# Scores of four chunks as three products of high and low parts, longer planned loads of q and k, and early weights from the thirtieth group on

## The chip, the cores and the metric

The kernel runs on one core of one Trainium2 chip. The metric is the device time of one execution in microseconds; the kernel before takes 701.42 us (median of 3 runs, 701.08 to 701.65).

The core has a matrix engine (TensorE, PE in the rows, with its weight loads shown apart as PEld), a vector engine (VectorE, DVE), a scalar engine (ScalarE, ACT), GpSimd (POOL) and SyncE (SP). POOL, SP and ACT also issue DMAs. Each engine works through its own list of instructions in order.

## What is computed

An attention with heads mixed before and after the softmax, and two feed-forward layers behind it:

```python
scores = scale * np.matmul(q, k.transpose(0, 1, 3, 2))      # 2 batches, 12 heads, 448 x 448, depth 64
scores = np.einsum('bhij,hg->bgij', scores, w_pre)
scores = scores - np.max(scores, axis=-1, keepdims=True)
attn = np.exp(scores)
attn = attn / (np.sum(attn, axis=-1, keepdims=True) + 1e-09)
attn = np.einsum('bhij,hg->bgij', attn, w_post)
x = np.matmul(attn, v)                                      # then 896 tokens x 768
h = x @ moe_w_in;  x = (h / (1 + np.exp(-1.702 * h))) @ moe_w_out
h = x @ moe2_w_in; x = (P(h) / (Q(h) + 1e-06)) @ moe2_w_out # P cubic, Q quadratic in |h|
```

The weights arrive as 64-bit numbers and are turned into float32 on the chip.

## The kernel before

**Attention.** The 448 query rows of a batch are cut into chunks of 120, 120, 120 and 88 rows: chunks 0 to 3 are of batch 0, chunks 4 to 7 of batch 1. The *scores* of a chunk (`scores`, L353) are computed for two heads at a time: q and k hold one head in partitions 0 to 63 and the other in 64 to 127, so that a pair is two float32 matmuls of 64 rows, on the two halves of the array, into the two banks of a tile `mm`. There are six pairs in a chunk. From chunk 2 on two pairs are issued one behind the other, as one block, so a chunk has three blocks. `scores_out` (L382, mostly on ACT) copies a pair to a tile S. SP then *regroups* (`regroup`, L391): one DMA for each group of 10 query rows (8 in the last group of a batch) moves all 12 heads of those rows from S into a tile T of 120 partitions. There are 90 groups, 12 for a chunk of 120 and 9 for one of 88, and ten T tiles.

For each group: `pre` (L397, PE) mixes the heads; `rowmax` (L403, DVE) and `expo` (L408, ACT) make the exponentials E; `norm` (L414, mostly DVE) the reciprocal of the sum and the scaled mixing matrix W and rest R; `post` (L443, PE, the matmuls of L449 and L452) mixes again and transposes; `post_out` (L454, mostly ACT) copies that to the tile AT of the chunk. When a chunk is done, `av` (L463, the matmuls of L475) multiplies with v and `x_part` (L485) splits the result into a rounded part (float32r) and the rest.

**Where S lies.** `place` (L314) gives each chunk a home for its scores: a tile S of its own, or one of two larger tiles that the feed-forward part needs only later (S2: the tag x1, S3: the tag wu). A chunk may write its scores to a place when all regroups of the chunk before it there are done (the mark `rgdone`, L597).

**Feed-forward.** `up` and `down` (L707, L775) take a weight and an activation as a high and a low float32r part each and sum three products: high by high, low by high, high by low (L715 to L717, L784 to L786).

**Weights.** A weight block is loaded by POOL (`w_load`, L659), taken through five conversions, one on ACT (`w_mag`, L667) and four on DVE (`w_bits`, L671), and split. The first 32 blocks of the second layer are converted ahead of time and stored to memory (`ahead`, L841); the first 12 of these (`EARLY`, L69) are spread over the attention groups, the others over the first layer. Six blocks of the first layer are also converted in the attention (`in_att`, L850).

**What sets the order.** A planner (`Plan`, L78) takes every step with its engine, its planned duration, its dependences, its buffers and a rank, runs a list schedule with these planned times when the program is built, and emits each engine's instructions in the order that comes out. Ranks count in groups: `RANK` (L34) says how many groups ahead of (negative) or behind its own group a step stands. A DMA step has a planned lag until it lands (`DMA_LAG`, L30). On the chip nothing is moved: an engine whose next instruction is not ready waits, and what stands behind it waits too.

The steps of the scores, the copies and the loads are made here:

```python
step(("kld", b, hp), "sp", 640 if b else 480, [("scdone", b * NC - 1)] if b else [], ...)      # L540
d0 = [("qld", ci), ("kld", b, hp | two)] + ([("sc", ci, hp - 1)] if two and hp % 2 else [])    # L562
step(("sc", ci, hp), "pe", 755, d0, rk, scores, ci, hp, take=["mm"], need=...)                 # L564
e = (NG - 12) * (j + 0.5) / EARLY + RANK["ahead"]                                              # L861
```

Of the kernel before, what the change touches and what calls it, by code (L numbers as in the profile page):

```python
# [29 lines left out]
DMA_LAG = 3500  # L30
RG_LAG = 5000
W_LAG = 5200

RANK = dict(k=-45, q=-45, v=-45, sc=-14, sco=-14, rg=-37, pre=-3, max=-3, exp=-6, n0=-9, n1=-9, n2=-4, n3=-4, post=1, phi=-4)  # L34
# [25 lines left out]
RB = 3  # L60
TAIL = 2
SINGLE = {0: (2, 3), 1: (0, 1)}
# [6 lines left out]
EARLY = 12  # L69
# [159 lines left out]
def row_groups(M):  # L229

    n = M // (2 * IS)
    left = M - 2 * n * IS
    out = []
    for g in range(2 * n):
        out.append((range(g, 2 * n * IS, 2 * n), g // 2 * IS + g % 2 * (n * IS + left)))
    return out + ([(range(M - left, M), n * IS)] if left else [])
# [3 lines left out]
def talking_heads_then_two_ffn(ctx: ExitStack, tc: tile.TileContext, q, k, v, wpre, wpost, win1, wout1, win2, wout2, ab, out):  # L240
# [12 lines left out]
    def psum(b, *n):  # L253
        return banks[b][plan.bank[n, b]]
# [59 lines left out]
    def place(ci):  # L314
        return ("S", "S2", "S3", "S2", "S", "S", "S3", "S")[ci]
# [7 lines left out]
    def load_k(b, hp):  # L323
        if hp == 0:
            t_["k", b] = ap1.tile([128, NP, S], F32, tag="k", name=f"k{b}")
        sp.dma_start(t_["k", b][:, hp], k[b, :, hp])

# [25 lines left out]
    def scores(ci, hp):  # L353
        b, c = chunks[ci]
        M = CHUNKS[c][1]
        p = t_["sc", ci, hp] = psum("mm", "sc", ci, hp)
        for o in range(2):
            r = slice(o * 64, o * 64 + 64)
            pe.matmul(p[:M, o, :S], t_["q", ci][r, hp, :M], t_["k", b][r, hp], start=True, stop=True)
# [80 lines left out]
    def alone(t):  # L440
        return t == last[groups[t][0]] and groups[t][1] % 2 == 0
# [11 lines left out]

    def post_out(t, eng):  # L454
        ci, gi, n, off = groups[t]
        if gi == 0:
            t_["AT", ci] = ap1.tile([128, NJ, H, IC], F32, tag="AT", bufs=2, name=f"AT{ci}")
        at = t_["AT", ci]
        p = t_["post", t][:, : NJ * IC].rearrange("p (j g i) -> p j g i", j=NJ, g=H)
        js = slice(0, NJ if gi % 2 or alone(t) else JM)  # L460
        cast(eng, at[:, js, :, off : off + n], p[:, js, :, :n])

    def av(ci, a):  # L463
        b, c = chunks[ci]
        M = CHUNKS[c][1]
        at, vt = t_["AT", ci], t_["v", b]
        y = t_["av", ci, a] = psum("bk", "av", ci, a)
        ev = M // (2 * IS) * IS
        parts = [(vt[:, jc], at[:, jc], 0, M) for jc in range(JM)]
        parts += [(vz[:, 0], at[:, JM, :, M - ev :], 0, ev), (vz[:, 1], at[:, JM, :, ev:], ev, M - ev)]  # L470
        for i in range(3):
            for k, (w, x, c0, n) in enumerate(parts):
                for o in range(2):
                    h = (3 * a + i) * 2 + o
                    pe.matmul(  # L475
                        y[o * 64 : o * 64 + 64, i * IC + c0 : i * IC + c0 + n],
                        w[:, h * D : h * D + D],
                        x[:, h, :n],
                        start=k == 0,
                        stop=k > JM,  # L480
                    )
# [3 lines left out]
    def x_part(ci, a, rest):  # L485
# [8 lines left out]
        else:  # L494
# [4 lines left out]
            **dict(mm=2, bk=4, T=TB, E=4, W=3, R=RB, sm=4, q=2, S=1, S2=1, S3=1, AT=2, k=1, v=1),  # L499
# [29 lines left out]
    def mark(name, deps, give):  # L529
        plan.add(name, (), deps, 0, give=give)  # L530
# [6 lines left out]
    for b in range(B):  # L537
        f0 = first[b * NC]
        for hp in range(NP):
            step(("kld", b, hp), "sp", 640 if b else 480, [("scdone", b * NC - 1)] if b else [], f0 + RANK["k"] + 0.01 * hp, load_k, b, hp, take=[] if hp else ["k"], lag=DMA_LAG)  # L540
        for jc in range(NJ):
            d0 = [("av", b * NC - 1, 1)] if b else [("vhold",)]
            step(("vld", b, jc), "sp" if b else "pool", 1280, d0, f0 + RANK["v"] + RANK["step_v"] * jc, load_v, b, jc, take=["v"] if b and not jc else [], lag=DMA_LAG)
    for ci, (b, c) in enumerate(chunks):
# [4 lines left out]
        step(("qld", ci), "sp" if ci else "act", 450 if ci else 890, d0, f0 + RANK["q"] - {1: 9.4, 2: 12.5}.get(ci, 0), load_q, ci, take=["q"], lag=DMA_LAG)  # L549
        for hp in range(NP):  # L550
# [11 lines left out]
            d0 = [("qld", ci), ("kld", b, hp | two)] + ([("sc", ci, hp - 1)] if two and hp % 2 else [])  # L562
            rk = -99 if two and hp % 2 else f0 + RANK["sc"] + 0.1 * hp
            step(("sc", ci, hp), "pe", 755, d0, rk, scores, ci, hp, take=["mm"], need=2 if two and hp % 2 == 0 else 1)  # L564
# [11 lines left out]
        mark(("scdone", ci), [("sc", ci, hp) for hp in range(NP)] + [("sc1", ci, hp) for hp in SINGLE.get(ci, ())], [("q", ("qld", ci))] + ([("k", ("kld", b, 0))] if end_b else []))  # L576
# [31 lines left out]
    mark(("late_s",), [("rgdone", 6)], [("wu", "late_s")] * 3)  # L608
# [246 lines left out]
    for key, us in uses.items():  # L855
# [3 lines left out]
        if key in ahead:  # L859
            j = ahead.index(key)  # L860
            e = (NG - 12) * (j + 0.5) / EARLY + RANK["ahead"]  # L861
# [21 lines left out]
    for L in range(2):  # L883
        for ft in range(NF):
            qq = ft // FQ
            for hf in range(2):
# [21 lines left out]
                if L == 0:  # L908
                    step(G, "act", 424, [u, ("exp", NG - 1)], p + RANK["gates"], gelu, key, take=["t0"], give=[bank])
                    step(("ghi",) + key, copying(S, "ghi0"), 0, [G] + g0, p + RANK["ghi0"], g_part, L, ft, hf, None, False, take=gt_)  # L910
                    step(("g",) + key, joining(S, "glo0"), 0, [("ghi",) + key], p + RANK["glo0"], g_part, L, ft, hf, None, True, give=[("t0", G)])
                else:
                    step(G, "act", 500, [u], p + RANK["gates"], cubic, key, take=["t0"])
# [109 lines left out]
```

## Time and profile of the kernel before

| | |
|---|---|
| median of the runs | 701.42 us (701.08 to 701.65, 3 runs) |
| the profiled execution | 700.76 us |
| its span, first to last instruction | 699.0 us |
| PE busy in the span | 694.0 us (99%) |
| DVE busy | 515.0 us (74%) |
| ACT busy | 459.5 us (66%) |
| POOL busy | 225.1 us (32%) |
| granted clock | 1.000 throughout |

The span is that of one execution, recorded by the profiler; 1.76 us of that execution's time lie outside it. Busy is the share of time in which an engine has an instruction in work; since matmuls overlap one another in the pipeline, a matmul's recorded duration is longer than the distance from its start to the next one's, and it is the distances between starts that add up to time on PE. The attention takes the first 234 us; the feed-forward layers the rest.

### The profile page before, as it was taken

Reading aid. Unit: us, or ns where it says so; the run is one execution under the profiler, and the core shown is the slowest. Engines: PE = TensorE matmul, PEld = TensorE weight load, DVE = VectorE, ACT = ScalarE, POOL = GpSimd, SP = SyncE. Lnnn points to the kernel's source line nnn. Section 1 sums busy time; section 2 is a strip of 40 time slices with the busy share of each in tenths; the row PEclk is TensorE's granted clock in tenths of the full one; section 3 lists DMA queues with packets and bytes.
Section 4 is the critical chain, followed back from the end, with each engine's and each line's share of the span. In section 5 each row is a group of like instructions: output and inputs, shape, how many; then the busy total and the mean of one; then the engine's idle time right before and its main releaser. Section 6 shows DMA issues by size and latency. Waiting matters only on the chain.

```text
span 699.0 us, 11972 instructions
## 1 busy us (share of the span) xinstructions
PE 694.0 (99%) x4292; PEld 594.1 (85%) x4292; DVE 515.0 (74%) x1101; ACT 459.5 (66%) x868; POOL 225.1 (32%) x361
## 2 busy tenths in 40 slices
PE   9999999999999999999999999999999999999998
PEld 4676767766769999999999999999999999999997
DVE  4688668567887596676787878859987387579952
ACT  4878677777685466665645554659898687488630
POOL 0411221120203255556465555412222222321320
PEclk9999999999999999999999999999999999999999
DMA  6886774864453487978889888755535544833563
GB/s 229 240 272 213 233 219 179 268 222 152 127 148 124 168 241 182 284 213 236 225 232 262 224 215 236 199 140 121 113 70 119 137 105 95 171 89 90 143 159 121
DMA packets 49961, 126.15 MB, mean 180 GB/s; under 512 B 7630, under 2 KB 21646, under 8 KB 49902
## 3 DMA queue, kind: packets, MB, share of 16 engines
q0 software_dynamic: 32480, 95.97, 51.1%
q1 hardware_dynamic: 17134, 29.05, 12.5%
q8 instruction: 34, 0.56, 0.3%
q10 hardware_dynamic: 288, 0.37, 0.1%
q14 instruction: 25, 0.20, 0.1%
HBM read 69.78 MB, written 13.24 MB: 119 GB/s over the span
## 4 chain that ended last, share of the span: by engine, by line
PE 70%; DMA 1%; ACT 0%; DVE 0%; issue 0%; ACTq 0%
PE bk L715 11%; PE mm L786 11%; PE mm L785 11%; PE mm L784 11%; PE bk L717 11%; PE bk L716 11%; PE bk L475 1%; PE bk L449 1%; DMA rawk<-in_wout_dram 1%; PE bk L400 1%; PE bk L452 0%; ACT wmk L669 0%; ACT AT L266 0%; DVE yt L274 0%; ACTq L669 0%
## 5 line engine op out<-in xcount | busy, mean ns | idle before, releaser
L785 PE MATMUL mm<-g,wd 128*128 128x448 f32 (+1 forms) x388 | 141.0, 363 | 0.0
L786 PE MATMUL mm<-g,wd 128*128 128x448 f32 (+1 forms) x388 | 141.0, 363 | 0.0
L784 PE MATMUL mm<-g,wd 128*128 128x448 f32 (+1 forms) x388 | 140.9, 363 | 0.0
L664 POOL DMA_DIRECT2D rawk<-in_win_dram x96 | 54.2, 593 | 172.9 <-ACT E L412 34.0
L449 PEld LDWEIGHTS bk<-W,E 120*128 120x128 f32 x540 | 72.2, 191 | 33.5 <-issue 21.6
L400 PE MATMUL bk<-T,wpr 120*120 120x448 f32 x180 | 81.5, 547 | 0.1
L785 PEld LDWEIGHTS mm<-g,wd 128*128 128x128 f32 x388 | 72.9, 188 | 5.7
L784 PEld LDWEIGHTS mm<-g,wd 128*128 128x128 f32 x388 | 72.9, 188 | 5.7
L786 PEld LDWEIGHTS mm<-g,wd 128*128 128x128 f32 x388 | 72.9, 188 | 5.6
L449 PE MATMUL bk<-W,E 120*128 120x120 f32 x540 | 76.0, 277 | 0.0
L406 DVE TENSOR_REDUCE sm<-bk 120x1 f32<-120x448 f32 (+1 forms) x90 | 55.8, 621 | 22.2 <-PE bk L400 20.8
L715 PE MATMUL bk<-xh,wu 128*128 128x448 f32 x192 | 70.5, 367 | 0.0
L715 PE MATMUL bk<-xn,wu 128*128 128x448 f32 x192 | 70.1, 365 | 0.0
L717 PE MATMUL bk<-xh,wu 128*128 128x448 f32 x192 | 70.1, 365 | 0.0
L716 PE MATMUL bk<-xn,wu 128*128 128x448 f32 x192 | 70.1, 365 | 0.0
L717 PE MATMUL bk<-xn,wu 128*128 128x448 f32 x192 | 70.1, 365 | 0.0
L716 PE MATMUL bk<-xh,wu 128*128 128x448 f32 x192 | 70.1, 365 | 0.0
L736 DVE SCALAR_TENSOR_TENSOR t<-t,cab,bk 128x448 f32<-128x448 f32 x64 | 43.5, 679 | 28.1 <-ACT t L732 21.4
L412 ACT ACTIVATE E<-bk,sm 120x448 f32<-120x448 f32 (+1 forms) x90 | 56.4, 627 | 6.9 <-PE bk L449 3.4
L266 ACT ACTIVATE AT<-bk 128x360 f32<-128x360 f32 (+2 forms) x83 | 43.3, 528 | 26.6 <-PE bk L452 15.7
L274 DVE TENSOR_TENSOR yt<-mm,yt 128x896 f32<-128x896 f32 (+2 forms) x44 | 40.4, 918 | 25.0 <-PE mm L786 24.8
L664 POOL DMA_DIRECT2D rawk<-in_wout_dram x56 | 32.3, 607 | 73.1 <-issue 19.9
(118 smaller groups left out, 1434.1 us busy)
## 6 DMA issues: line engine op xcount, KB each, us to landing
rawk<-in_win_dram POOLq DMA_DIRECT2D x96, 256.0 KB, 4.0
T<-S SPq DMA_DIRECT2D x88, 210.0 KB
rawk<-in_wout_dram POOLq DMA_DIRECT2D x56, 256.0 KB, 4.2
raw<-in_wout_dram POOLq DMA_DIRECT2D x40, 256.0 KB, 4.7
wd<-wm POOLq DMA_DIRECT2D x19, 256.0 KB, 4.9
d1u<-wmk POOLq DMA_DIRECT2D x24, 192.0 KB, 4.2
rawk<-d1u POOLq DMA_DIRECT2D x12, 384.0 KB, 4.1
wu<-rawk POOLq DMA_DIRECT2D x12, 384.0 KB, 4.2
```

Source lines behind the costliest of these rows:

```text
L400: pe.matmul(p[:K, :S], wpr[:K, :K], t_["T", t][:K], start=True, stop=True)
L406: dve.tensor_reduce(t_["sm", t][:K, 0:1], t_["pre", t][:K, :S], AX.X, ALU.max, negate=True)
L412: act.activation(t_["E", t][:K], t_["pre", t][:K, :S], AF.Exp, bias=sm[:K, 0:1], scale=1.0, accum_out=sm[:K, 1:2])
L449: pe.matmul(o, t_["E", t][:K, jc * 128 : jc * 128 + 128], t_["W", t][:K], start=True, stop=True)
L664: pool.dma_start(r[:, c : c + 256], src[:, c : c + 256])
L715: pe.matmul(p[:, :S], w[:, 0, ws], x[:, 0, kk], start=kk == 0, stop=False)
L716: pe.matmul(p[:, :S], w[:, 1, ws], x[:, 0, kk], start=False, stop=False)
L717: pe.matmul(p[:, :S], w[:, 0, ws], x[:, 1, kk], start=False, stop=kk == KK - 1)
L736: dve.scalar_tensor_tensor(t, t, col(i), t_[("h",) + key][:, :S], ALU.add, ALU.mult)
L784: pe.matmul(p[:, hf, :n], w[:, 0, ms], gt[:, 0, i, cs], start=i == 0, stop=False)
L785: pe.matmul(p[:, hf, :n], w[:, 1, ms], gt[:, 0, i, cs], start=False, stop=False)
L786: pe.matmul(p[:, hf, :n], w[:, 0, ms], gt[:, 1, i, cs], start=False, stop=i == FQ - 1)
```

## The change

- **Scores of chunks 3 to 6** (`SPLIT`): q and k are split into a high part rounded to float32r and a low part, the rest. ACT makes the high parts (`khi`, `qhi`), DVE the low ones (`klo`, `qlo`). Each pair is then three float32r products per half instead of one float32 product per half: high by high, high by low, low by high. The planned duration on PE is 610 instead of 755. k is split in six steps for each batch, q in one for each chunk.
- **Room.** The split k of batch 0 lies in S2's tile, that of batch 1 in S3's. `PLACES` changes: chunks 0, 3, 5, 6 and 7 use S, chunks 1 and 4 S2, chunk 2 S3. The split q has one buffer, as large as what the two AT tiles lose: AT holds, for each head, seven strips of half a chunk's columns instead of four of a chunk's, and the two rows of `vz` are exchanged to match, as is the order of the rows of q.
- **Loads.** k of batch 1 may be loaded when k of batch 0 has been split and chunks 0 to 2 are scored (it was: when chunk 3 was scored). The planned lag of a load is 9500 for q from chunk 3 on and 7500 for k of batch 1 (both were 3500).
- **Early weights.** 13 blocks instead of 12, with ranks spread from group 30 on instead of from the first.
- **Planned time** of the two first activations behind a table load: 1300 more. The first weights of the first layer get their tile when the scores of chunk 6 are done (it was: when its regroups were).

```diff
+Q_LAG, K_LAG = 9500, 7500
+TABLE = 1300
...
-RANK = dict(k=-45, q=-45, v=-45, sc=-14, sco=-14, rg=-37, pre=-3, max=-3, exp=-6, n0=-9, n1=-9, n2=-4, n3=-4, post=1, phi=-4)
+RANK = dict(kh=-15, k=-45, q=-45, v=-45, sc=-14, sco=-14, rg=-37, pre=-3, max=-3, exp=-6, n0=-9, n1=-9, n2=-4, n3=-4, post=1, phi=-4)
...
+STRIPS = 2 * JM + 1
+SPLIT = (3, 4, 5, 6)
+QB = 1
+WAIT = (1,), (2,)
+PLACES = "S", "S2", "S3", "S", "S2", "S", "S", "S"
...
-EARLY = 12
+EARLY = 13
+AFTER = 30
...
-        out.append((range(g, 2 * n * IS, 2 * n), g // 2 * IS + g % 2 * (n * IS + left)))
+        out.append((range(g, 2 * n * IS, 2 * n), g // 2 * IS + (1 - g % 2) * (n * IS + left)))
...
-        return ("S", "S2", "S3", "S2", "S", "S", "S3", "S")[ci]
+        return PLACES[ci]
...
+
+    def q_part(ci, rest):
+        if rest:
+            sub(dve, t_["qh", ci][:, 1], t_["q", ci], f(t_["qh", ci][:, 0]))
+        else:
+            t_["qh", ci] = ap1.tile([128, 2, NP, IC], F32R, tag="qh", bufs=QB, name=f"qh{ci}")
+            cast(act, t_["qh", ci][:, 0], t_["q", ci])
+
+    def k_part(b, hp, rest):
+        if rest:
+            sub(dve, t_["kh", b][:, 1, hp], t_["k", b][:, hp], f(t_["kh", b][:, 0, hp]))
+            return
+        if hp == 0 and b == 0:
+            t_["kh", b] = keep.tile([128, 2, KK, S], F32R, tag="x1", name="kh0")
+        elif hp == 0:
+            x = keep.tile([128, H * S], F32R, tag="wu", name="kh1")
+            t_["kh", b] = x.rearrange("p (a h s) -> p a h s", a=2, h=NP)
+        cast(act, t_["kh", b][:, 0, hp], t_["k", b][:, hp])
...
+        if ci in SPLIT:
+            qs, kh = t_["qh", ci], t_["kh", b]
+            terms = ((0, 0), (0, 1), (1, 0))
+            for i, (x, y) in enumerate(terms):
+                for o in range(2):
+                    r = slice(o * 64, o * 64 + 64)
+                    pe.matmul(p[:M, o, :S], qs[r, x, hp, :M], kh[r, y, hp], start=i == 0, stop=i == 2)
+            return
...
+    def strip(ci):
+        M = CHUNKS[chunks[ci][1]][1]
+        return M - M // (2 * IS) * IS
+
...
-            t_["AT", ci] = ap1.tile([128, NJ, H, IC], F32, tag="AT", bufs=2, name=f"AT{ci}")
-        at = t_["AT", ci]
-        p = t_["post", t][:, : NJ * IC].rearrange("p (j g i) -> p j g i", j=NJ, g=H)
-        js = slice(0, NJ if gi % 2 or alone(t) else JM)
-        cast(eng, at[:, js, :, off : off + n], p[:, js, :, :n])
+            t_["AT", ci] = ap1.tile([128, H * STRIPS * IC // 2], F32, tag="AT", bufs=2, name=f"AT{ci}")
+        w = strip(ci)
+        at = t_["AT", ci][:, : H * STRIPS * w].rearrange("p (g s u) -> p g s u", s=STRIPS, u=w)
+        p = t_["post", t][:, : NJ * IC].rearrange("p (j g i) -> p g j i", j=NJ, g=H)
+        if gi % 2 or alone(t):
+            cast(eng, at[:, :, ::2, off : off + n], p[:, :, :, :n])
+        else:
+            cast(eng, at[:, :, 1::2, off - w : off - w + n], p[:, :, :JM, :n])
...
-        at, vt = t_["AT", ci], t_["v", b]
+        vt = t_["v", b]
...
-        ev = M // (2 * IS) * IS
-        parts = [(vt[:, jc], at[:, jc], 0, M) for jc in range(JM)]
-        parts += [(vz[:, 0], at[:, JM, :, M - ev :], 0, ev), (vz[:, 1], at[:, JM, :, ev:], ev, M - ev)]
+        st = strip(ci)
+        at = t_["AT", ci][:, : H * STRIPS * st].rearrange("p (g c) -> p g c", g=H)
+        parts = [(vt[:, jc], at[:, :, 2 * jc * st :], 0, M) for jc in range(JM)]
+        parts += [(vz[:, 1], at[:, :, 2 * JM * st :], 0, st), (vz[:, 0], at[:, :, 2 * JM * st :], st, M - st)]
...
-            **dict(mm=2, bk=4, T=TB, E=4, W=3, R=RB, sm=4, q=2, S=1, S2=1, S3=1, AT=2, k=1, v=1),
+            **dict(mm=2, bk=4, T=TB, E=4, W=3, R=RB, sm=4, q=2, qh=QB, S=1, S2=1, S3=1, AT=2, k=1, v=1),
...
-            step(("kld", b, hp), "sp", 640 if b else 480, [("scdone", b * NC - 1)] if b else [], f0 + RANK["k"] + 0.01 * hp, load_k, b, hp, take=[] if hp else ["k"], lag=DMA_LAG)
+            step(("kld", b, hp), "sp", 640 if b else 480, ([("kld", b, 0)] if hp else [("scdone", 0)]) if b else [], f0 + RANK["k"] + 0.01 * hp, load_k, b, hp, take=[] if hp else ["k"], lag=K_LAG if b else DMA_LAG)
+        mine = [ci for ci in SPLIT if ci // NC == b]
+        for hp in range(NP if mine else 0):
+            rk = first[mine[0]] + RANK["kh"] + 0.1 * hp
+            step(("khi", b, hp), "act", 585, [("kld", b, hp)] + ([("khi", b, 0)] if hp else [("rgdone", c) for c in WAIT[b]]), rk, k_part, b, hp, False, take=[] if hp else ["S3" if b else "S2"])
+            step(("klo", b, hp), "dve", 560, [("khi", b, hp)], rk + 0.05, k_part, b, hp, True)
+        plain = [ci for ci in range(b * NC, b * NC + NC) if ci not in SPLIT]
+        mark(("kend", b), [("klo", b, hp) for hp in range(NP if mine else 0)] + [("scdone", ci) for ci in plain], [("k", ("kld", b, 0))])
+        if mine:
+            mark(("khend", b), [("scdone", ci) for ci in mine], [("S3" if b else "S2", ("khi", b, 0))])
...
-        step(("qld", ci), "sp" if ci else "act", 450 if ci else 890, d0, f0 + RANK["q"] - {1: 9.4, 2: 12.5}.get(ci, 0), load_q, ci, take=["q"], lag=DMA_LAG)
+        step(("qld", ci), "sp" if ci else "act", 450 if ci else 890, d0, f0 + RANK["q"] - {1: 9.4, 2: 12.5}.get(ci, 0), load_q, ci, take=["q"], lag=Q_LAG if ci > 2 else DMA_LAG)
+        if ci in SPLIT:
+            rk = f0 + RANK["kh"]
+            step(("qhi", ci), "act", 800, [("qld", ci)], rk, q_part, ci, False, take=["qh"])
+            step(("qlo", ci), "dve", 910, [("qhi", ci)], rk, q_part, ci, True, give=[("q", ("qld", ci))])
...
-            d0 = [("qld", ci), ("kld", b, hp | two)] + ([("sc", ci, hp - 1)] if two and hp % 2 else [])
+            split = ci in SPLIT
+            d0 = [("qlo", ci), ("klo", b, hp | two)] if split else [("qld", ci), ("kld", b, hp | two)]
+            d0 += ([("sc", ci, hp - 1)] if two and hp % 2 else [])
...
-            step(("sc", ci, hp), "pe", 755, d0, rk, scores, ci, hp, take=["mm"], need=2 if two and hp % 2 == 0 else 1)
+            step(("sc", ci, hp), "pe", 610 if split else 755, d0, rk, scores, ci, hp, take=["mm"], need=2 if two and hp % 2 == 0 else 1)
...
-        mark(("scdone", ci), [("sc", ci, hp) for hp in range(NP)] + [("sc1", ci, hp) for hp in SINGLE.get(ci, ())], [("q", ("qld", ci))] + ([("k", ("kld", b, 0))] if end_b else []))
+        mark(("scdone", ci), [("sc", ci, hp) for hp in range(NP)] + [("sc1", ci, hp) for hp in SINGLE.get(ci, ())], [("qh", ("qhi", ci)) if split else ("q", ("qld", ci))])
...
-    mark(("late_s",), [("rgdone", 6)], [("wu", "late_s")] * 3)
+    mark(("late_s",), [("khend", 1)], [("wu", "late_s")] * 3)
...
-            e = (NG - 12) * (j + 0.5) / EARLY + RANK["ahead"]
+            e = AFTER + (NG - 12 - AFTER) * (j + 0.5) / EARLY + RANK["ahead"]
...
-                    step(G, "act", 424, [u, ("exp", NG - 1)], p + RANK["gates"], gelu, key, take=["t0"], give=[bank])
+                    step(G, "act", 424 + TABLE * (ft == hf == 0), [u, ("exp", NG - 1)], p + RANK["gates"], gelu, key, take=["t0"], give=[bank])
...
-                    step(G, "act", 500, [u], p + RANK["gates"], cubic, key, take=["t0"])
+                    step(G, "act", 500 + TABLE * (ft == hf == 0), [u], p + RANK["gates"], cubic, key, take=["t0"])
...
```

## Rows read from the trace of the kernel before

**Rows 1.** The page's totals: busy us, share of the span, instructions, by engine

```profile
PE 694.0 (99%) x4292; PEld 594.1 (85%) x4292; DVE 515.0 (74%) x1101; ACT 459.5 (66%) x868; POOL 225.1 (32%) x361
```

**Rows 2.** Waits of PE: line, releaser, us in total, times, longest us

```profile
PE bk L260 <- DVE warm L279: 1.2, 1, 1.2
PE mm L359 <- ACT S L266: 0.3, 1, 0.3
```

**Rows 3.** Windows: stretch, length, each engine's busy us (instructions), granted clock, DMA share, GB/s

```profile
20.00:100.00 80.00, 80.00 (x627) 55.30 (x627) 61.51 (x206) 61.43 (x146) 22.25 (x42) 1.00 0.74 228
100.00:230.00 130.00, 129.86 (x1210) 97.30 (x1212) 95.09 (x302) 91.53 (x217) 23.25 (x43) 1.00 0.55 183
180.00:200.00 20.00, 20.00 (x204) 15.29 (x204) 18.59 (x53) 15.02 (x37) 3.21 (x6) 1.00 0.50 151
240.00:690.00 450.00, 450.00 (x2222) 417.00 (x2221) 341.51 (x563) 289.84 (x479) 175.97 (x268) 1.00 0.66 172
```

**Rows 4.** Timeline, 65.6 to 68.2: start us, us, engine, line, output<-inputs, shape, records

```profile
65.31 0.92 PE L400 MATMUL bk<-T,wpr 120*120 120x448 f32 x2
...
66.15 0.23 PEld L359 LDWEIGHTS mm<-k,q 64*88 64x88 f32 x4 [0.66 <-issue]
66.15 1.74 PE L359 MATMUL mm<-k,q 64*88 64x448 f32 x8
...
66.60 0.16 PEld L359 LDWEIGHTS mm<-k,q 64*88 64x88 f32 x2 [0.22 <-issue]
...
66.98 0.16 PEld L359 LDWEIGHTS mm<-k,q 64*88 64x88 f32 x2 [0.22 <-issue]
...
67.82 0.59 PE L449 MATMUL bk<-W,E 120*128 120x120 f32 x3
```

**Rows 5.** Timeline of PE, 299.70 to 302.14: first and last of thirteen starts

```profile
299.70 0.37 PE L716 MATMUL bk<-xh,wu 128*128 128x448 f32 x1
...
302.14 0.36 PE L785 MATMUL mm<-g,wd 128*128 128x448 f32 x1
```

**Rows 6.** Timeline of PE in the product with v: two neighbouring stretches

```profile
73.44 0.40 PE L475 MATMUL bk<-AT,vz 128*64 128x60 f32 x8
73.66 0.79 PE L475 MATMUL bk<-AT,v 128*64 128x120 f32 x12
```

**Rows 7.** Groups by line, 234 to 690: count, busy us, mean ns

```profile
L266 ACT ACTIVATE g<-t 128x448 fp32r<-128x448 f32 x61 | 35.0, 574 | 8.0 <-DVE t L756 7.1
...
L266 ACT ACTIVATE wu<-rawk 128x768 fp32r<-128x768 f32 x10 | 8.3, 834 | 0.0
...
L271 DVE TENSOR_TENSOR g<-t,g 128x448 fp32r<-128x448 f32 x64 | 39.7, 621 | 12.5 <-ACT g L266 11.8
...
L271 DVE TENSOR_TENSOR wu<-wmk,wu 128x768 fp32r<-128x768 f32 x1 | 1.0, 953 | 0.0
```

**Rows 8.** Windows of the converted weights alone (tile wmk): busy us (instructions)

```profile
20.00:85.00 65.00, 11.94 (x16) 3.64 (x4) 4.31 (x8) 1.00 0.75 237
85.00:100.00 15.00, 5.18 (x8) 1.56 (x2) 1.61 (x3) 1.00 0.67 186
100.00:230.00 130.00, 36.00 (x53) 10.64 (x13) 5.96 (x11) 1.00 0.55 183
```

**Rows 9.** The chain of waits, 196 to 207: start us, us, what

```profile
197.35 6.37 DMA rawk<-in_wout_dram
...
203.83 0.67 ACT wmk L669
...
205.02 1.76 PE bk L400 x4
```

**Rows 10.** Timeline of SP, 116 to 134: regroups around the scores of chunk 5

```profile
116.09 0.77 SPq L395 DMA_DIRECT2D T<-S  x1
...
133.21 0.86 SPq L395 DMA_DIRECT2D T<-S  x1
```

**Rows 11.** Timeline of PE at 144.54: the first pre of chunk 5

```profile
144.54 0.92 PE L400 MATMUL bk<-T,wpr 120*120 120x448 f32 x2
```

## The prediction

> **What bounds the kernel now.** I read the totals first: PE is busy 99% of the span, DVE 74%, ACT 66% [rows 1]. A busy PE may still be waiting inside its pipeline, so the second view is who PE waited for: in the whole span 1.2 us for the first memset, and behind that no wait on another engine above 0.3 us [rows 2]. [...] So time is the sum of PE's own work nearly from end to end: an edit that takes work from PE is worth its full length, and an edit on another engine costs nothing until PE waits for it. The reader should also see in [rows 3] how close that is: DVE has 18.59 of 20 us of work from 180 to 200 and PE still does not wait.
>
> **What a block of scores costs now.** The fourth view is the timeline around one block of two pairs [rows 4]. Its eight matmul records (two passes for each float32 product, for each half, for each pair) start at 66.15 and what follows starts at 67.82. The two halves run side by side: loads come in twos, at 66.60 and at 66.98, so a pass of both halves takes 0.38 us, and the block four passes, 1.52. The other 0.15 us are the way in, where no load stands ahead of the first pass; they stay.
>
> **What it costs after.** A block of float32r has two pairs times three products: six passes. No row shows float32r on half the array, so I bound a pass.
> - Float32r on the whole array: from 299.70 to 302.14 there are twelve starts, 0.203 us each [rows 5].
> - Below: half a float32 pass, 0.19, if float32r on half the array hides its load as completely as float32 does there.
> - Above: the halves one behind the other, 2 x 0.203 = 0.41.
>
> I take 0.203: it is the same data type, length and engine, and that halves of the array load and run side by side is seen in float32 twice: in [rows 4], and with column halves in the product with v, where eight short matmuls, each behind a load of its own, take from 73.44 to 73.66 together [rows 6]. Six passes are 1.22 us, 0.30 less than 1.52. Chunks 3 to 6 have three blocks each, twelve: **3.6 us less on PE**. With 0.19 it is 12 x (1.52 - 1.14) = 4.6 less; with 0.41 it is 12 x (2.46 - 1.52) = 11.3 more. The number of blocks and so of changes between halves and the whole array is the same.
>
> **What is added off PE.** The high parts on ACT: twelve steps of 448 columns at 0.574, as the same cast takes in the feed-forward part, and four of 720 columns at about 0.8 (768 take 0.834): 6.9 + 3.2 = 10.1 us. The low parts on DVE: twelve at 0.621 and four at about 0.9 (768 take 0.953): 7.5 + 3.6 = 11.1 us [rows 7]. I cost these at nothing: what hides them is the slack above. They are spread: both splits of k and the first two of q have ranks 21 to 30, and the groups of those ranks run before 100 us, the other two of q behind.
>
> **Early weights.** Before 85 us DVE spends 11.9 us on four blocks, from 85 to 100 another 5.2 on two, and 36.0 from 100 to 230 [rows 8]. The new ranks start at 30 + 48 x 0.5 / 13 + 8 = 39.8, about where those two stand (37.3 and 43.8). So four blocks, and the thirteenth, go into 100 to 230: 5 x 3.0 = 15 us of DVE, 5 x 0.9 = 4.5 of ACT. DVE in that stretch: 95.1 + 15 + 1.8 for two low parts of q = 112 us in 127, 88%. From 20 to 100 it is 61.5 - 11.9 + 9.3 = 59 of 80. ACT is 91.5 + 4.5 + 1.6 = 98 of 127 behind 100 (77%), and 61.4 - 3.6 + 8.5 = 66 of 80 before (83%). Both stay under the 93% that DVE bears from 180 to 200 without a wait on PE. POOL issues the loads closer together, from 23 of 130 us busy at a DMA share of 0.55 [rows 3]: room for both. Cost zero, unless an instruction stands in the wrong place (second rival). One block fewer in the feed-forward part frees engines that PE does not wait for: zero.
>
> **Waits, order and room.** A load's planned lag moves its readers back in the lists and changes no transfer; `kld` of batch 1 waits for the low parts of k of batch 0, not for the scores of chunk 3, so SP, where the regroups stand behind that wait, is held earlier and not longer. The first `khi` of a batch waits on ACT for the regroups of chunk 1 or 2, behind which exponentials and copies are queued; these regroups have ranks 37 groups ahead of their own, and the rank of `khi` is 15 ahead of chunks 3 and 4, two chunks later, so I expect nothing there. The new AT has the same runs of ten columns in and out, and its smaller size only saves room: zero. The planned 1300 for the table load and the earlier tile for the first weights move work that PE does not wait for.
>
> **The sum.** The profiled execution took 700.76 us (span 699.0 and 1.76 around it): 700.76 - 3.6 = 697.2. It lies 0.66 under the median of the runs, against which the result will stand: 701.42 - 3.6 = **697.8**.
>
> **The rivals.**
> 1. *The halves don't hide their loads, slower.* The point that decides is a pass of 1.52 / 6 = 0.25 us. If a half's next load waits for its own matmul, a pass is 0.203 and a load as recorded, 0.16 [rows 4]: 0.36, a block 2.18, 12 x 0.66 = 7.9 more: 709; fully one behind the other, 713. For it: a float32r pass is about half as long, so the same loads have half the cover. Against: in [rows 4] the first four loads stand within 0.23 us while the first pass of both halves is still running until 66.60, so a half takes its next load under its own matmul. [...] Chance 6%.
> 2. *The crowding behind group 30.* An ACT or DVE instruction that waits for a weight block holds the exponentials behind it. The chain shows it once: a weight load in flight from 197.35, ACT's conversion at 203.83 only, then ACT's copy, then PE at 205.02 [rows 9]; that is the 0.14 that PE lacks in [rows 3]. With 13 blocks in a shorter stretch and DVE at 88% this can come more often. Five to twelve such places of 0.3 give back 1.5 to 3.6: 699.3 to 701.4; one that stops the groups for longer costs more. Against: attention steps have lower ranks than the early weights and are served first. Chance 25%: 18% for a time from 699.6 to 702.8, 7% above.
> 3. *One place for chunks 5, 6 and 7.* Scores of a chunk may be copied only when the last regroup of the chunk before is done, twice in a row now. The trace has one such turn: chunk 4's last regroup at 116.09, chunk 5's first at 133.21 [rows 10], its first `pre` at 144.54 [rows 11]. So 11 us are in hand, less the landing. It costs something only if the turn takes 8 us or so longer; then PE waits for the rest, twice. Chance 3%, about 703 to 708.
> 4. *A pass of 0.19*, and fewer places where a load has no cover: under 696.5. Chance 4%.
>
> The forecast has the other 62%, with 696.5 to 699.6 as its own range.
>
> **How the numbers follow.** About 0.2%, 1.4 us, is what a measurement of this kernel can tell from no change, so faster means under 700.0 and slower above 702.8. Faster: 62 + 4 + 3 of the second rival = 69%. Same: the other 15% of its near part. Slower: 6 + 7 + 3 = 16%. From 696.5 to 702.5 lie 62% and nearly all of the 18%: 80%.
>
> **What would show it.** Right: the starts inside a block of chunks 3 to 6 stand 0.19 to 0.21 us apart for each pass of both halves; PE waits for nothing above 0.5 us; the feed-forward part begins 3 to 4 us earlier and lasts as long as before. Wrong: passes above 0.25; an idle PE from 100 to 234, released by ACT's copies or exponentials with a DVE or ACT conversion just ahead of these; a first regroup of chunk 6 or 7 less than 4 us ahead of its `pre`; a feed-forward part that starts earlier and has new waits for its first weights.

## The result, and the profile after

| | before | after |
|---|---|---|
| median of 20 runs each (us) | 701.33 | 705.33 |
| lowest to highest (us) | 700.64 to 702.01 | 702.24 to 709.63 |
| profiled execution, its span (us) | 700.76, 699.0 | 705.9, 703.9 |
| mean granted clock of TensorE | 1.000 | 0.995 |

The changed kernel takes 1.0056 times as long (95% interval 1.0044 to 1.0068): 4.0 us slower, where 3.6 less was predicted. Its runs also scatter over 7 us, those of before over 1.4.

The totals and the waits of PE come first, as in [rows 1] and [rows 2]; the second fence gives the waits as us in total, times and the longest.

```profile
PE 695.7 (99%) x4340; PEld 599.8 (85%) x4340; DVE 529.6 (75%) x1126; ACT 463.0 (66%) x875; POOL 225.7 (32%) x361
```

```profile
PE bk L434 <- DVE xh L279: 2.1, 1, 2.1
PE bk L483 <- DVE xh L279: 1.2, 1, 1.2
PE bk L268 <- DVE warm L287: 1.2, 1, 1.2
PE mm L393 <- ACT S L274: 0.3, 1, 0.3
```

PE is still busy 99% of the span, and a reader who stopped there would see nothing. The waits show two new ones, 2.1 and 1.2 us; L434 is the old L400 (`pre`), L483 the old L449 (`post`). The windows, against [rows 3], say where they lie (busy us of PE, PEld, DVE, ACT, POOL; granted clock, DMA share, GB/s):

```profile
20.00:100.00 80.00, 76.53 (x609) 55.71 (x608) 60.77 (x197) 60.22 (x147) 18.05 (x34) 0.96 0.71 218
100.00:230.00 130.00, 130.00 (x1224) 98.64 (x1225) 104.71 (x328) 97.14 (x225) 25.58 (x49) 1.00 0.56 183
240.00:690.00 450.00, 449.95 (x2221) 416.61 (x2220) 346.60 (x571) 289.61 (x478) 175.50 (x266) 1.00 0.66 171
```

All of it is between 20 and 100 us: there PE lacks 3.47 us that it did not lack before, and the clock is 0.96. From 100 to 230 PE is full, with DVE at 104.71 of 130; the feed-forward part is as before.

**The blocks of scores did get shorter.** This is the timeline of PE around the first block of two pairs in chunk 4, before and after; both have 120 rows, where the block of [rows 4], in chunk 3, has 88:

```profile
89.06 1.77 PE L359 MATMUL mm<-k,q 64*120 64x448 f32 x8
90.75 0.48 PE L449 MATMUL bk<-W,E 120*128 120x120 f32 x2
```

```profile
94.36 1.49 PE L389 MATMUL mm<-kh,qh 64*120 64x448 f32 x12
95.77 0.48 PE L483 MATMUL bk<-W,E 120*128 120x120 f32 x2
```

and of the loads after:

```profile
94.36 1.10 PEld L389 LDWEIGHTS mm<-kh,qh 64*120 64x120 f32 x12
```

Twelve records now, and all twelve loads lie within 1.10 us. The block takes 95.77 - 94.36 = 1.41 us instead of 90.75 - 89.06 = 1.69. The second block of chunk 3, the chunk of [rows 4], goes from 60.01 to 61.39, 1.38 us instead of 1.67. Adding up PE's time from each start to the next by kind of work, over the whole profiled execution:

| PE's time (us) | before | after | difference |
|---|---|---|---|
| scores | 41.0 | 37.7 | -3.3 |
| `pre` and `post` | 143.0 | 151.0 | +8.0 |
| product with v | 39.9 | 39.9 | 0.0 |
| feed-forward | 467.5 | 467.8 | +0.3 |

So the gain is there, and 8 us are lost in two places of the attention part.

**The two places, from ACT's side.** Timeline of ACT at the first one (in brackets the idle time ahead of an instruction and who ended it):

```profile
44.67 0.18 ACT L446 ACTIVATION_READ_ACCUMULATOR E<-bk,sm 120x1 f32 x1
48.16 0.58 ACT L274 ACTIVATE kh<-k 128x448 fp32r<-128x448 f32 x1 [3.31 <-DMA cab<-in_ab_dram]
48.64 0.45 ACT L274 ACTIVATE xh<-bk 128x360 fp32r<-128x360 f32 x1
```

and at the second:

```profile
75.35 0.21 ACT L446 ACTIVATION_READ_ACCUMULATOR E<-bk,sm 120x1 f32 x1
79.28 0.58 ACT L274 ACTIVATE kh<-k 128x448 fp32r<-128x448 f32 x1 [3.72 <-DMA T<-S]
79.76 0.45 ACT L274 ACTIVATE xh<-bk 128x360 fp32r<-128x360 f32 x1
...
82.22 0.45 ACT L274 ACTIVATE xh<-bk 128x360 fp32r<-128x360 f32 x1
82.57 0.39 ACT L470 ACTIVATE W<-wsrc,sm 120x120 f32<-120x120 f32 x1
```

ACT stands for 3.31 and 3.72 us in front of the first `khi` of each batch. In the code that step waits for its load of k and for all regroups of chunk 1 (batch 0) or chunk 2 (batch 1). Behind it in ACT's list are the high parts of x (`xh`), the copies and the exponentials, and behind these DVE's low parts, PE's `post` and `pre`. At the second place the regroup (`T<-S`) is named as the releaser. At the first it is a load of constants (`cab`) that `khi` does not read. The trace also has the times at which each transfer counts up its semaphore, and these settle it. The last regroup of chunk 1 was issued at 39.24 and its last count came at 47.85, and ACT's wait for that semaphore ended at 47.87. The last regroup of chunk 2 was issued at 69.38 and had landed at 79.26, and `khi` starts at 79.28. In the kernel before, the last regroup of chunk 1 landed as late, 8.9 us after its issue, and ACT waited for no regroup there: the change did not make the landing late, it put a reader in front of it.

PE at the second place, and the windows from there on:

```profile
79.97 0.92 PE L434 MATMUL bk<-T,wpr 120*120 120x448 f32 x2
81.01 0.93 PE L483 MATMUL bk<-W,E 120*128 120x120 f32 x6
84.06 1.85 PE L434 MATMUL bk<-T,wpr 120*120 120x448 f32 x2 [2.12 <-DVE xh L279]
85.70 1.47 PE L483 MATMUL bk<-W,E 120*128 120x120 f32 x6
```

```profile
83.60:90.40 6.80, 6.34 (x19) 4.62 (x20) 4.83 (x13) 3.23 (x8) 0.00 (x0) 0.50 0.17 39
90.40:97.20 6.80, 6.80 (x42) 4.69 (x42) 5.60 (x17) 5.76 (x16) 2.68 (x5) 1.00 0.74 224
```

PE waits 2.12 us, and from 83.6 on the granted clock is 0.50 for 6.8 us: two `pre` that took 0.92 take 1.85. PE is busy for 6.34 of these 6.8 us, which at 1.00 would be 3.2 us of work: 3.2 are lost. Together: the two waits 2.12 + 1.23 = 3.35, the half clock 3.2, and some 1.5 in smaller gaps beside them make the 8 us. Of the 3.31 and 3.72 us that ACT stood, PE felt a part; the clock then more than doubled the second one.

### The profile page after: what moved, and what is told of

Same layout as the page of the kernel before. It is cut to its first block, busy times and chain, and to the rows that moved or that the text cites. A ratio compares the mean times of both kernels' runs of the same rounds, so it can differ in the third digit from the quotient of the medians.

```text
span 703.9 us, 12082 instructions
## 1 busy us (share of the span) xinstructions
PE 695.7 (99%) x4340; PEld 599.8 (85%) x4340; DVE 529.6 (75%) x1126; ACT 463.0 (66%) x875; POOL 225.7 (32%) x361
## 4 chain that ended last, share of the span: by engine, by line
PE 92%; ACT 3%; DMA 3%; issue 1%; DVE 1%; POOL 0%; SPq 0%; POOLq 0%
PE mm L843 11%; PE mm L841 11%; PE mm L842 11%; PE bk L773 10%; PE bk L774 10%; PE bk L772 10%; PE bk L434 10%; PE bk L483 9%; PE bk L517 4%; PE mm L389 2%; PE mm L393 2%; PE bk L486 1%; DMA cab<-in_ab_dram 1%; DMA q<-in_q_dram 1%; DMA wu<-rawk 1%
## 5 line engine op out<-in xcount | busy, mean ns | idle before, releaser
L483 PEld LDWEIGHTS bk<-W,E 120*128 120x128 f32 x540 | 73.1, 194 | 35.8 <-issue 20.3
L721 POOL DMA_DIRECT2D rawk<-in_win_dram x84 | 46.3, 560 | 153.0 <-ACT W L470 39.8
L434 PE MATMUL bk<-T,wpr 120*120 120x448 f32 x180 | 84.2, 558 | 2.1 <-DVE xh L279 2.1
L483 PE MATMUL bk<-W,E 120*128 120x120 f32 x540 | 77.5, 281 | 1.4 <-DVE xh L279 1.2
L721 POOL DMA_DIRECT2D rawk<-in_wout_dram x64 | 35.9, 582 | 100.6 <-ACT R L464 19.7
L274 ACT ACTIVATE AT<-bk 128x480 f32<-128x480 f32 (+2 forms) x80 | 41.9, 527 | 28.9 <-PE bk L486 18.4
```

Of the source, the lines that this page charges most:

```text
L434: pe.matmul(p[:K, :S], wpr[:K, :K], t_["T", t][:K], start=True, stop=True)
L483: pe.matmul(o, t_["E", t][:K, jc * 128 : jc * 128 + 128], t_["W", t][:K], start=True, stop=True)
L721: pool.dma_start(r[:, c : c + 256], src[:, c : c + 256])
```

## Experiments

The theory that the trace suggests: the split of k stands too early in ACT's list, ahead of the landing of the regroup that it waits for, and all of the loss comes from that. The rivals: the early weights crowd the stretch behind group 30 (second rival of the prediction); the other edits (lags, ranks, places) cost it; the split itself is not worth what the trace says. Unless a diff says that it is made from before, an experiment is made from the kernel after. No experiment leaves out a part of the computation.

### The order on ACT, later and earlier

The planner takes it that a regroup has landed `RG_LAG` (5000 ns) after its issue, and sets `khi` into ACT's list by that. No instruction has this lag in it: it only tells the planner when the readers can go, and the planner then writes its lists in another order. Longer for the two regroups in question (the last of chunk 1 and of chunk 2):

```diff
 step(("rg", t), "sp", 1200,
...
-    lag=RG_LAG if ci else 2500)
+    lag={last[1]: 9500, last[2]: 11500}.get(t, RG_LAG if ci else 2500))
```

> The changed kernel with one planned number altered: the regroups of the last group of chunk 1 and of chunk 2, for which the first high part of k of each batch waits, are planned to land 9500 and 11500 behind their issue instead of 5000. Nothing that is computed changes, and no wait is taken away. Theory A (the list order puts the first high part of k on ACT ahead of the landing of these regroups, ACT stands 3.3 and 3.7 us, the copies of the product with v behind it come late, and PE stands): the two waits of ACT shrink below 1 us, PE waits below 1 us in all, its clock stays at 1.00 from 80 to 100, and the time is 698 to 700, 5 to 7 under the changed kernel. Rival B (the early weights crowd ACT and DVE behind group 30): the waits move or stay and the time stays at 704 to 706. Rival C (three products cost more than the one pass): 704 to 706 as well.

Measured: 700.11 us (699.37 to 705.74, 10 runs), ratio 1.0006 (0.9985 to 1.0027); the profiled execution has a span of 698.0. ACT no longer waits for a `kh`, the clock is 1.00, and PE's time in `pre` and `post` is back at 143.0. So the 8 us went with the order alone. Six of the runs lie at 699.4 to 700.1, four, of which none was profiled, at 702.4 to 705.7; the median is just above the expected range. What kept the profiled one (699.74) from the 697.8 of the prediction is a new wait in the second feed-forward layer, 1.5 us with what follows it:

```profile
PE mm L841 <- ACT yt L274: 0.9, 1, 0.9
```

The same lags shorter:

```diff
-    lag=RG_LAG if ci else 2500)
+    lag={last[1]: 2500, last[2]: 2500}.get(t, RG_LAG if ci else 2500))
```

> The same two regroups are planned to land 2500 behind their issue instead of 5000, so the first high part of k stands earlier in ACT's list (about 0.5 us for batch 0, 3.6 us for batch 1 by the planned times). Theory A: ACT waits longer, by about as much, some 7 us for the second, PE stands longer, and the time rises to 707 to 711. Rivals B and C: no change, 704 to 706.

Measured: 709.88 us (706.17 to 711.54, 4 runs), ratio 1.0116 (1.0084 to 1.0148). Waits of ACT and of PE:

```profile
ACT kh L274 <- DMA q<-in_q_dram: 5.5, 1, 5.5
ACT kh L274 <- DMA cab<-in_ab_dram: 4.6, 1, 4.6
```

```profile
PE bk L483 <- DVE xh L279: 2.3, 2, 1.2
PE bk L434 <- ACT E L446: 2.0, 1, 2.0
PE bk L434 <- DVE xh L279: 2.0, 2, 1.5
```

ACT stands longer (4.6 and 5.5 instead of 3.3 and 3.7, where 0.5 and 3.6 more had been expected), PE waits 6.3 us instead of 3.3, and the time goes up by 4.6. The view names other loads, but the two regroups landed at 49.27 and 82.41, and the two `khi` start at 49.59 and 82.51. The half clock, again 6.8 us, has moved to the first place (0.50 from 53.6 to 60.4). The cost follows the place of `khi` in both directions.

### Which of the two places

```diff
-    lag=RG_LAG if ci else 2500)
+    lag={last[1]: 9500, last[2]: 5000}.get(t, RG_LAG if ci else 2500))
```

> Only the last regroup of chunk 1 is planned later (9500 instead of 5000); that of chunk 2 is as in the changed kernel. Theory A: the wait of ACT at 45 to 48 us is gone with its 1.4 us of PE; the one at 76 to 79 us, the larger with its idle 2.3 us and the 6.8 us at half clock behind it, becomes shorter, because the list behind it moves as well: 698 to 702. If the first wait is the cause of the second by what it delays, the second is gone too: below 699.

Measured: **697.30 us** (697.08 to 697.87, 4 runs), ratio 0.9946 (0.9934 to 0.9959), span 695.4. Waits of PE, ACT's first `kh` of the two batches, and PE's window:

```profile
PE bk L268 <- DVE warm L287: 1.2, 1, 1.2
PE mm L393 <- ACT S L274: 0.3, 1, 0.3
```

```profile
51.52 0.57 ACT L274 ACTIVATE kh<-k 128x448 fp32r<-128x448 f32 x1
...
76.35 0.57 ACT L274 ACTIVATE kh<-k 128x448 fp32r<-128x448 f32 x1
```

```profile
20.00:100.00 80.00, 80.00 (x655) 58.78 (x653) 68.29 (x221) 65.74 (x158) 18.72 (x35) 1.00 0.76 230
```

Both `kh` start without a wait, though only the first was moved: at 76.35, 2.9 us earlier than in the kernel after, the second finds its regroup landed. That regroup was issued at 65.00 instead of 69.38 and landed at 73.06. This is the last case of the expectation: without the first wait the second is gone too. The lists behind the first place have moved as well, so how much of this is the wait's own effect is not separated. PE's waits are those of [rows 2] again. The other half:

```diff
-    lag=RG_LAG if ci else 2500)
+    lag={last[1]: 5000, last[2]: 11500}.get(t, RG_LAG if ci else 2500))
```

> Only the last regroup of chunk 2 is planned later (11500 instead of 5000). Theory A: the wait at 45 to 48 us and its 1.4 us of PE stay, the second and the half clock are gone: 699 to 701.5.

Measured: 701.27 us (699.09 to 702.38, 10 runs), ratio 0.9998 (0.9988 to 1.0008), span 699.8. The first wait is there, and the half clock now follows the first place:

```profile
ACT kh L274 <- DMA T<-S: 3.9, 1, 3.9
```

```profile
50.00:53.10 3.10, 1.36 (x5) 0.58 (x5) 3.10 (x8) 3.10 (x8) 0.00 (x0) 1.00 0.58 189
53.10:56.50 3.40, 3.40 (x14) 1.87 (x14) 2.94 (x9) 2.43 (x8) 0.00 (x0) 0.50 0.17 63
```

So the first wait, with the half clock behind it, is worth 701.27 - 697.30 = 4.0 us where the second is gone, and each of the two edits removes the second one. With the first in place nothing more is to be had from the second's lag; moving both, with `khi` one rank later, gives less:

```diff
-RANK = dict(kh=-15, ...
+RANK = dict(kh=-14, ...
...
-    lag=RG_LAG if ci else 2500)
+    lag={last[1]: 9500, last[2]: 10500}.get(t, RG_LAG if ci else 2500))
```

> The changed kernel with the two regroups planned to land 9500 and 10500 behind their issue, and the rank of the high and low parts at 14 groups ahead instead of 15, so that both first high parts of k stand later in ACT's list. Theory A: ACT waits for neither regroup, PE for nothing above 0.5 us, the scores cost 37.7 to 38.3 us of PE against 41.0 before the change, and the time is 697.5 to 699, faster than before the change. If the parts themselves crowd ACT and DVE (rival B), 700 or more.

Measured: 699.07 us (697.92 to 702.06, 12 runs), ratio 0.9971 (0.9962 to 0.9981), span 696.1; no `kh` waits. Scores, `pre` and `post` take 181.1 us, against 180.3 with the first lag alone: the rest of the planner's order shifts with each such number, by about a microsecond.

### Why the regroup lands late

In the kernel after, SP issues two regroups from 39.24 on, and ACT goes on at 48.16. Another kernel holds the first weight loads back, by tying them to the exponential of group 20 instead of group 8:

```diff
-act.activation(f(tiles["raw"][i][:1, :1]), t_["E", 8][:1, :1], AF.Copy)
+act.activation(f(tiles["raw"][i][:1, :1]), t_["E", 20][:1, :1], AF.Copy)
...
-step(("hold",), "act", 300, [("exp", 8)], -40, hold_raw)
+step(("hold",), "act", 300, [("exp", 20)], -40, hold_raw)
```

> The changed kernel with the first weight loads held until the exponentials of group 20 are made instead of group 8, so that from 32 to 48 us no weight block is on the way; the planned time of the first high part of k of batch 0 stays as it was. Theory A as to where the wait comes from: with the DMA queues less full the regroups land as planned, and the wait of ACT ahead of that part (3.3 us, till 48.2) shrinks below 1 us with nothing else moved. If the regroups are late for another reason, the wait stays at 3 us or so. The total is not the point: the early weights come later and the feed-forward part may wait for them (700 to 710).

Measured: 712.36 us (one run). From 30 to 48 us, first the kernel after, then this one; and its regroups and its first `kh`:

```profile
30.00:48.00 18.00, 18.00 (x197) 14.22 (x195) 11.70 (x44) 12.01 (x30) 3.23 (x6) 1.00 0.81 257
```

```profile
30.00:48.00 18.00, 18.00 (x181) 13.84 (x181) 12.76 (x49) 13.78 (x35) 0.00 (x0) 1.00 0.58 194
```

```profile
39.99 2.19 SPq L429 DMA_DIRECT2D T<-S  x2
```

```profile
44.69 0.58 ACT L274 ACTIVATE kh<-k 128x448 fp32r<-128x448 f32 x1
```

The pair is issued 0.75 us later than in the kernel after and `kh` starts at 44.69 without a wait, 3.5 us earlier. The DMA share in that stretch is 0.58 instead of 0.81, with no weight load by POOL instead of six. By its semaphore the last regroup of chunk 1 landed 4.4 us after its issue, in the kernel after 8.6 us; there the six weight blocks landed between 39.5 and 44.4, just ahead of it. With one execution at each load, this bears out, and no more, that the regroup was late because it shared the DMA engines with the weights. It is no cure. The weights now crowd the second place: six are issued from 58.82 on, the last regroup of chunk 2 takes 8.2 us to land, and ACT waits 2.0 us in batch 1 (the view names a load of k, but the regroup landed at 73.57, and `khi` starts at 73.80). The feed-forward part takes 476.6 us instead of 467.8 (see the last section); of the regroup of chunk 1 this run tells something, of the total nothing.

### The other edits alone

The scores as before, everything else as after:

```diff
-SPLIT = (3, 4, 5, 6)
+SPLIT = ()
...
-    mark(("late_s",), [("khend", 1)], [("wu", "late_s")] * 3)
+    mark(("late_s",), [("rgdone", 2)], [("wu", "late_s")] * 3)
```

> The changed kernel with no chunk split: all scores in one float32 product, no high and low parts; places of the scores, planned loads, the strips of AT and the early weights stay as changed. Theory A: neither the gain of 3.6 on PE nor the waits behind the high parts: 700.5 to 702.5, as before the change. Rival B: the waits from the early weights stay and the gain is missing: 706 to 709. Rival C: 701 to 702.

Measured: 702.33 us (701.98 to 702.93, 10 runs), ratio 1.0016 (1.0006 to 1.0025), span 700.9. With no `khi` there is no wait of 3 us and little scatter; the other edits cost 1.2 us by the medians. In the profiled execution, 0.9 of its 1.9 us are scores (41.9 instead of 41.0) and 0.9 are four more of the planner's filler matmuls on `warm`. The 0.9 of scores lie in the first two blocks of chunk 0, at the very start of the execution (3.1 + 1.5 us instead of 1.8 + 1.9). The edits do not touch these blocks, and the first of them takes 1.8 to 3.1 us in the kernels of this text.

The early weights as before, the rest as after:

```diff
-EARLY = 13
-AFTER = 30
+EARLY = 12
+AFTER = 0
```

> The changed kernel with the early weights as they were, 12 blocks spread from the first group on. Theory A: the waits of ACT for the regroups stay, 703 to 707. Rival B: the loss of time goes with the crowding, 698 to 700.

Measured: 706.12 us (704.21 to 707.57, 4 runs), ratio 1.0068 (1.0045 to 1.0092), span 705.5. ACT still waits 2.9 us for a `kh`, once, and `pre` and `post` take 145.3 us: the wait comes without the new early weights too. Another 5.9 us of this span are a feed-forward part of 473.4 us, which no expectation had; so it is the wait that speaks here, and not the time.

The early weights of after alone, in the kernel before:

```diff
-EARLY = 12
+EARLY = 13
...
-e = (NG - 12) * (j + 0.5) / EARLY + RANK["ahead"]
+e = 30 + (NG - 12 - 30) * (j + 0.5) / EARLY + RANK["ahead"]
```

> The kernel before with the early weights of the change alone: 13 blocks, ranks from the thirtieth group on; scores, loads and places as before. Theory A: nothing that PE waits for, 700.5 to 702. Rival B (crowding): 703 or more.

Measured: 706.99 us (702.00 to 707.24, 5 runs), ratio 1.0066 (1.0043 to 1.0089), span 705.2. PE's waits are those of [rows 2], and scores, `pre`, `post` and the product with v take 224.2 us, against 223.9 before: no crowding, though the time is one that the expectation gave to it. 5.1 us are lost in the feed-forward part (472.6), with no wait and at a clock of 1.00. The windows of 460 to 500 us, before and here:

```profile
460.00:500.00 40.00, 40.00 (x199) 37.05 (x198) 31.43 (x55) 32.73 (x56) 9.20 (x13) 1.00 0.51 113
```

```profile
460.00:500.00 40.00, 40.00 (x195) 36.34 (x194) 31.80 (x55) 32.30 (x56) 7.00 (x10) 1.00 0.39 85
```

195 matmuls instead of 199 in the same 40 us (those cut by an edge are counted): 0.2067 us from start to start instead of 0.2027. I suspected the planner's filler matmuls, and left those out that it sets behind 400 us:

```diff
 (the change of b_early, and)
-if now >= self.fill_from and b and ...
+if self.fill_from <= now < 400000 and b and ...
```

> The kernel before with the early weights of the change alone, and without the two filling matmuls that the plan puts at 438 us. With the filling matmuls this kernel's trace has 0.2067 us from start to start behind 443 us instead of 0.2027, and 707 us. If the filling matmuls set the slower pace, it is gone and the time is 701 to 702.5; if the short gap at 443 us sets it, 705 to 707.5 stay.

Measured: 706.51 us (701.83 to 707.33, 9 runs), ratio 1.0061 (1.0039 to 1.0084). Three runs lie at 701.8 to 702.4 and six at 706.5 to 707.3, none between; the profiled one, 702.4, has 199 matmuls in that window:

```profile
460.00:500.00 40.00, 40.00 (x199) 37.06 (x199) 31.92 (x55) 32.41 (x57) 7.15 (x10) 1.00 0.39 87
```

The profiled execution of b_early has both paces, one after the other (see the last section), and the times of either program fall into two groups some 4.5 us apart. So one and the same program most likely runs its feed-forward part at either of two paces, and the fillers left out here don't choose; that the pace makes the groups is not shown, since one execution of each was profiled. At the quicker pace the early weights cost about 1 us. What chooses the pace is open.

## Why the prediction was wrong, step by step

**The step that failed** is the sentence on the waits: the first `khi` of a batch waits on ACT for the regroups of chunk 1 or 2, "these regroups have ranks 37 groups ahead of their own, and the rank of `khi` is 15 ahead of chunks 3 and 4, two chunks later, so I expect nothing there." I named the wait, what is queued behind it and who would feel it, and then priced it by ranks. A rank says in what order steps that are ready are taken, not when a step becomes ready: the last regroup of chunk 1 was issued at 39.24, since by the code it needs a free tile `T`, and landed at 47.85; ACT's list had reached `khi` at 44.85. The price was 3.31 and 3.72 us on ACT, 3.35 on PE, and 8.0 on PE with the half clock and the smaller gaps. I had no term for the clock: that the granted clock fell to 0.50 at 84 us cost 3.2 where the wait itself cost 2.1. With the planned landing of one regroup mended (the experiment of the first lag) the kernel takes 697.30, near the 697.8 of the forecast. The 3.6 us by which that span is shorter than the one of before are not quite the sum's own, though, and that they equal it is in part luck: 3.4 come from the twelve blocks, 0.7 from `pre` and `post` (142.3 instead of 143.0), where I had nothing, and some 0.4 go back into the scores of chunk 0 at the start.

The measured time lies among the slower ones, to which the prediction gave 16%, but none of the three causes that it named for them occurred.

**PE as the bound: right.** Where nothing stops it, 20 to 100 us is 80.00 of 80 again, in the experiment of the first lag as in [rows 3].

**The pass and the block: right, the size a little off.** Twelve loads in 1.10 us, none waiting for the end of the matmul before it, so passes of 0.20 us as the forecast had it. A block gives back 0.28 (120 rows) or 0.29 (88 rows), not 0.30: the float32 pass that I read as 0.38 is 0.376 from start to start, so four take 1.50 and not 1.52, while the rest of the block, 0.17 at 88 rows, stays. The twelve blocks together give back 3.4 us, not 3.6. The sum over all scores shrinks by 2.8 to 3.3 in most of the kernels, since chunk 0, which the change leaves as it was, takes longer or shorter at the start of each execution.

**First rival (halves don't hide their loads): fell.** The deciding pass was 0.25, measured is 0.20. The same halves of the array take their next load while they run, in float32r (in the block at 94.36 the loads of the second pass stand 0.10 us behind the start of the first, and that pass runs for 0.30) as in float32 ([rows 4]).

**The work off PE: the sizes right.** Groups by line, 20 to 235 us (count, busy us, mean ns, idle ahead):

```profile
L274 ACT ACTIVATE kh<-k 128x448 fp32r<-128x448 f32 x12 | 6.5, 568 | 7.0 <-DMA T<-S 3.7 <-DMA cab<-in_ab_dram 3.3
L279 DVE TENSOR_TENSOR kh<-k,kh 128x448 fp32r<-128x448 f32 x12 | 7.1, 619 | 5.7 <-ACT kh L274 5.7
```

568 and 619 ns against the 574 and 621 of [rows 7]; the 720-column ones take 799 and 898. The work itself costs nothing, as said; its place does.

**Second rival (crowding): fell as a cause of the loss.** DVE has 104.71 of 130 us from 100 to 230, 81% and not 88%, and PE is full there; b_early shows no new wait. My 88% was too high because the blocks didn't move as far as I had read from their ranks: DVE still spends 7.14 us on them before 85 us (11.94 in [rows 8]), since POOL has room then (busy for 13.28 of the 65 us from 20 to 85) and takes a late rank as soon as it is all there is. It is the same mistake as above, with a harmless result.

**Third rival (one place for chunks 5 to 7): did not occur.** No wait stands there. **Fourth (a pass of 0.19): no.**

**The other edits at zero: off by about 1 us**, as plain (1.2) and b_early at its quicker pace indicate; what in them costs it is not shown.

What stays open is the scatter of the kernel after, 702.24 to 709.63: two paces of the feed-forward part and a wait whose length hangs on a transfer would make it, but only the profiled execution was looked into. The mean granted clock, which each run has, points at a part of it: the four runs at 0.995, the profiled one among them, took 705.9 to 707.7 us, the two at 1.000 702.2 and 703.6.

## What to carry to other kernels

When a change adds a wait to an in-order engine, price it by two clock times, when the engine's list gets there and when the awaited transfer lands at the load of that stretch; a rank or a priority is not a time. A planner that counts on 5.0 us for a landing that takes 8.6 to 9.9 should be given the landing as measured: one such number, moved from 5000 to 9500, turned 705.33 us into 697.30, faster than both kernels. And a wait that starves PE may cost twice, as the one at 84 us did: once as itself, 2.12 us, and once as a stretch at a clock of 0.50, 3.2 us.

## What was new of the hardware

- **Two paces at full clock.** Whole-array float32r matmuls of 448 columns start 0.2027 us apart in most of the profiled executions and 0.2067 in others, at a granted clock of 1.00 in both. Around 443 us the profiled execution of b_early shows starts 0.27 to 0.31 apart at single places, and the pace changes there, from 0.2027 ahead of it to 0.2067 behind (timeline of PE):

```profile
442.73 0.36 PE L784 MATMUL mm<-g,wd 128*128 128x448 f32 x1
442.93 0.37 PE L785 MATMUL mm<-g,wd 128*128 128x448 f32 x1
443.14 0.36 PE L786 MATMUL mm<-g,wd 128*128 128x448 f32 x1
443.41 0.44 PE L784 MATMUL mm<-g,wd 128*128 128x448 f32 x1
443.69 0.37 PE L785 MATMUL mm<-g,wd 128*128 128x448 f32 x1
```

  In the profiled execution of b_nofill gaps stand at 443 and 446 us too, no smaller (0.51 and 0.34 from start to start), and the pace stays at 0.2027, so a gap alone does not decide it. In the experiment with the old early weights the slower pace ends where 14 filler matmuls run, at 502.6 us; what sets the pace is open. It cost 5 to 9 us where it lasted (5.1 in b_early, 5.9 with the old early weights, 8.8 in hold), more than the whole change was to bring.
- **A 210 KB regroup that lands in 4.4 us at a DMA share of 0.58 takes 8.6 us at 0.81** (30 to 48 us, hold and the kernel after), the pair being issued at the same speed by SP (2.19 us).
- **The half clock came on after a stretch in which PE, though never idle for more than 2.1 us, had little to do**: eight matmuls start from 79.97 to 84.06 in the kernel after, five records in 3.1 us at the first place of the experiment of the second lag. It lasted 6.8 and 3.4 us. The wait of 1.23 us at the first place of the kernel after was not followed by it (1.00 from 50.0 to 56.5 us).
